# Second tap sums from superblock 10 on, and a tap sum tied to a later tile, in a dynamic convolution with a two-matmul block

## The chip, the cores and the metric

The kernel runs on one core of a Trainium2 chip. The metric is device time in microseconds (us) of one execution. The core has TensorE (PE, matmuls; PEld are its weight loads), VectorE (DVE), ScalarE (ACT), GpSimd (POOL) and SyncE (SP, which here only issues DMA transfers). GpSimd issues DMA transfers too. All transfers run on the same 16 DMA engines of the core.

## The reference

The first stage is a causal convolution with 7 taps whose weights differ by token and head (softmax over the taps); the second is two matmuls with `h - tanh(h)` between them.

```python
def _attn_ref(x, weight_gen):          # x: 8 x 4096 x 192; weight_gen: 8 x 4096 x 8 heads x 7 taps
    w = softmax of weight_gen over the 7 taps
    x_pad = np.concatenate([np.zeros((B, 6, D)), x], axis=1)
    x_unf = x_pad[:, idx, :]           # the 7 last tokens of each token, by head
    out = np.einsum('bshk,bskhg->bshg', w, x_unf)
...
def _moe_ref(x, w_in, w_out):          # x: 32768 x 192; w_in: 192 x 2048; w_out: 2048 x 192
    h = x @ w_in
    g = h - np.tanh(h)
    return g @ w_out
```

Inputs and output are float32.

## The kernel before, in words

The 32768 tokens are cut into 32 superblocks of 1024 tokens (8 tokens in each of 128 partitions). Stage n of the main loop (`for n in range(1, NTOT)`) is the time in which superblock n goes through the first matmul; it is cut into 16 f tiles of 128 columns, indexed 0 to 15. The program's order is written out by hand (`manual_schedule`): each engine runs its instructions in the order of the program, and waits only where data or a dependency added by `order` demands it.

**An f tile.** `gemm1(n, f)`: TensorE does 6 matmuls of 512 columns into `ph` (L478), ScalarE takes `tanh` of it (L491, `th`), VectorE subtracts (L492, `gt`). Between the f tiles TensorE does the second matmul of superblock n-1 in pieces (L546, `obank`), doled out by the plan's `pairs`; ScalarE copies its results out (L565), and SP stores them (`out_sb`, L569).

**The taps of a superblock.** `products(n + 2)` is called in stage n at f tile 1 and gives the seven tap products of superblock n+2. GpSimd multiplies taps 0 to 3 into a tile `pa` in two instructions (L263), later taps 4 to 6 into `pb` (L263). The tokens that VectorE takes off GpSimd (`help`, L291 and L263 on DVE: the last token of taps 0 and 1 at f tile 3 of stage n-2, and for superblocks 9 to 14 one more at f tile 12 of stage n-3) make the first of the two `pa` instructions shorter: 2688 elements with one token taken off, 2304 with two.

**Sums by DMA.** GpSimd then issues an adding DMA (`dma_sum`, L252) that adds `pb` to `pa[0:3]`; this is the three-tap sum, and four products are left. For the superblocks in `TWO_SUMS` (13 to 31) a second adding DMA adds `pa[2:4]` to `pa[0:2]`, and two products are left. It is issued by `second_sum(n - 1)` behind the `pa` products of the next superblock, and waits for the landing of the three-tap sum. The rest of the products (pb and the three-tap sum) is the function `rest`, called in stage n at the f tile of the last help (3). So GpSimd's queue for steady superblocks is: two `pa` products of m, second sum of m-1, `pb` product of m, three-tap sum of m, and the same for m+1.

**Transposes.** In stage n TensorE turns the products that are left of superblock n+1 by matmuls with a unit matrix that add them up in PSUM (`transposes`, `conv_sums`, L418, `pc`): 24 matmuls for each product. ScalarE copies the result to `convT` (L444), which stage n+1 needs from its first f tile on. The plan says where they stand: in `STEADY`, 32 of 48 (or 64 of 96) at f tile 13 and the rest at f tile 14 (`t2=(13, 0)`, `t1=(14, 8)`); in `DOUBLE`, used for stages 4 to 11, at f tiles 11 and 15.

**Loads.** `loads(n)` at f tile 1 issues from SP the x of superblock n+3 (`load_x`, L150; it waits for GpSimd's first `pa` product of superblock n+2 by `x_after`) and the tap weights of a later superblock (`load_wg`, L136). x lies in a ring of two places. SP's queue holds x loads, weight loads, out stores and, for each fourth superblock, a zero row for the halo (L160), each behind the one before.

Of the kernel before, what the change touches and what calls it, by code (L numbers as in the profile page):

```python
# [8 lines left out]
FP32 = mybir.dt.float32  # L9
# [7 lines left out]
def kernel(  # L17
# [8 lines left out]
    nc = tc.nc  # L26
# [5 lines left out]
    P = nc.NUM_PARTITIONS  # L32
    R = P // 2
# [5 lines left out]
    HT = TOK // 2  # L39
    NSB = S // TOK  # L40
    NTOT = B * NSB
    NFT = F // P
    NC = D // R
    KA, KH = 4, 2
    PART = (2, 3)
    TWO_SUMS = (13, 14, 15, 16, 17, 18, 19, 20, 21, 22, 23, 24, 25, 26, 27, 28, 29, 30, 31)
    THREE = ()
    AHEAD = 4
    STORE_FIRST = 8
    EXTRA = (5, 9, 11, 13)  # L50

    HELP = {n: ((n - 2, 3, 2),) for n in range(4, 32)} | {n: ((n - 2, 3, 2), (n - 3, 12, 2)) for n in range(9, 15)}
    CUTS0 = [0, 2, 4]
    LAST_TAP = (4, 5, 6, 7, 8)
    X_LATE = ()
# [24 lines left out]
    psum_h = ctx.enter_context(tc.tile_pool(name="psum_h", bufs=3, space=bass.MemoryType.PSUM))  # L80
    psum_o = ctx.enter_context(tc.tile_pool(name="psum_o", bufs=1, space=bass.MemoryType.PSUM))

    ident = const.tile([P, P], BF16, name="ident")
# [24 lines left out]
    last_sub = {}  # L108
# [5 lines left out]
    ramp_scale = {}  # L114
    tap_of = {}
    pace_of = {}

    def order(inst, other, reason):
        tc.add_manual_dep(
            inst.ins,  # L120
            other.ins.name,
            mybir.DependencyInfo(mybir.DependencyClass.Sync, mybir.DependencyReason.DATA),
            reason=reason,
        )
# [9 lines left out]
    def load_wg(n):  # L134
        wg_t = wgpool.tile([P, J, H, K], FP32, name="wg_t")
        nc.sync.dma_start(out=wg_t[:], in_=tokens(weight_gen.rearrange("b s h k -> (b s) h k"), n))  # L136
        wg_of[n] = wg_t

    def load_x(n, behind=None):

        wide = 2 * J if n < 2 else J
        at = {0: 0, 1: J}.get(n, 0 if n % 2 else HALO + J)
        if n == 2:
            x_t = npool.tile([P, 2 * J, D], FP32, name="x2", tag="spare")[:, 0 : HALO + J]
        else:
            x_t = x_ring[:, at : at + HALO + J]

        def rows(p0, p1, r0=0, r1=HALO + J):
            first = x[0, 0:1]
            return nc.sync.dma_start(  # L150
                out=x_t[p0:p1, r0:r1, :],
                in_=bass.AP(
                    tensor=first.tensor,
                    offset=first.offset + (n * TOK - (TOK - J if n == 1 else 0) + p0 * wide - HALO + r0) * D,
                    ap=[[wide * D, p1 - p0], [D, r1 - r0], [1, D]],
                ),
            )

        def no_halo():
            nc.sync.dma_start(  # L160
                out=x_t[0:1, 0:HALO, :],
                in_=zero[:].rearrange("o (h d) -> o h d", h=1).to_broadcast([1, HALO, D]),
            )

        if n == 0:
            rows(0, P, HALO, HALO + J)
            rows(16, P, 0, HALO)
            rows(1, 16, 0, HALO)
            no_halo()
        else:  # L170
            dma = rows(0, P, HALO if n == 1 else 0)
            if behind is not None:
                order(dma, behind, "order of the loads")
            if n % NSB == 0:
                halo_of[n] = no_halo
        x_of[n] = x_t
# [74 lines left out]
    def dma_sum(out, in_):  # L251
        return nc.gpsimd.dma_start(  # L252
            out=out.rearrange("p k j d -> p k (j d)"),
            in_=in_.rearrange("p k j d -> p k (j d)"),
            accum_op=mybir.AluOpType.add,
            max_dma_last_dim=2 * J * D,
        )
# [36 lines left out]
    def products(n, taps=None, sums=None, hooks={}):  # L294

        x_t = x_of.pop(n)
        wsm, wsm_v, e_t, zr = wsm_of.pop(n)
        if e_t is not None:
            scale(nc.gpsimd, wsm[:], e_t, zr[:])

        pa = held[n][2] if n in held else papool.tile([P, KA, J, D], BF16, name="pa")
        held[n] = (x_t, wsm, pa)
        if n == 1:

            last = [opool.tile([P, 2, J, D], BF16, name="pb1", tag="out_sb") for _ in range(2)]
            home = [(pa, 0, KA), (last[0], KA, KA + 2), (last[1], KA + 2, K)]
        else:
            pb = pbpool.tile([P, K - KA, J, D], BF16, name="pb")
            home = [(pa, 0, KA), (pb, KA, K)]

        def prod(k0, k1):
            for t, a, b in home:
                if a <= k0 and k1 <= b:
                    return t[:, k0 - a : k1 - a]

        def mul(eng, k0, k1, j0=0, j1=J):
            w = wsm_v if eng is nc.vector else wsm[:]
            return tap_product(eng, prod(k0, k1), x_t, w[:, j0:j1, :, k0:k1], (1, K), k0, k1, j0, j1)

        def parts(*ks):  # L320
            return [[prod(k, k + 1)[:, 0] for k in ks]] * NC

        if taps is not None:
            for eng, k0, k1, j0, j1 in taps:
                m = mul(eng, k0, k1, j0, j1)
                if eng is nc.vector:
                    tap_of.setdefault((n, k0), m)
                if j1 == 1:
                    first_halo[0] = m
                if k0 in hooks:  # L330
                    hooks[k0]()
            prods_of[n] = parts(*sums)
            return

        end = KA - 1 if n in LAST_TAP else KA
        left = [J - sum(kh > k for _, _, kh in HELP.get(n, ())) for k in range(KA)]
        for j, k in {(j, k) for j, k, _ in ACT_OPS.get(n, ())}:
            left[k] = min(left[k], j)

        def most(k0, k1):  # L340
            return mul(nc.gpsimd, k0, k1, 0, left[k0])

        cuts = [0, *(k for k in range(1, end) if left[k] != left[k - 1]), end]
        if cuts == [0, end]:
            cuts = sorted({*(c for c in CUTS0 if c <= end), end})
        first = None
        for k0, k1 in zip(cuts, cuts[1:]):
            m = most(k0, k1)
            first = first or m
        x_after[n + 1] = first  # L350
        second_sum(n - 1)
        def rest():
            if n in PART:
                dma_sum(pa[:, 0:2], pa[:, 2:4])
            if n - 1 in whole:
                mul(nc.gpsimd, KA, K - 1)
                third_sum(n - 1)
                mul(nc.gpsimd, K - 1, K)
            else:
                mul(nc.gpsimd, KA, K)  # L360
            if n in PART:
                prods_of[n] = parts(4, 5, 6, 0, 1)
            else:
                dma_sum(pa[:, 0:3], pb[:, 0:3])
                if n in LAST_TAP:
                    most(KA - 1, KA)
                if n in TWO_SUMS:
                    to_sum[n] = pa
                    prods_of[n] = parts(0, 1)
                else:  # L370
                    prods_of[n] = parts(3, 0, 1, 2)
                if n == NTOT - 1:
                    second_sum(n)
                    third_sum(n)

        return rest
# [277 lines left out]
    V, G_, A = nc.vector, nc.gpsimd, nc.scalar  # L654
    load_wg(0)
    load_x(0)
    load_wg(1)
    softmax_exp(0)
    for c0, c1 in W_CUTS:
# [89 lines left out]
    STEADY = dict(pairs=(5, 11, 0, 16, 4, 12, 6, 10, 0, 6, 10, 8, 8, 8, 8, 16), t1=(14, 8), t2=(13, 0), scale=14, sums=(1, 13))  # L749
    FIRST = dict(pairs=(4, 12, 0, 16, 1, 15, 0, 16, 0, 16, 0, 13, 3, 0, 16, 16), t1=(15, 2), t2=(11, 10), scale=15, sums=(1, 2, 3, 4, 8, 10))  # L750
    APART = dict(pairs=(4, 12, 0, 16, 0, 16, 4, 12, 0, 16, 4, 12, 0, 6, 10, 16), t1=(15, 5), t2=(10, 2), scale=15, sums=(7, 10))
    APART_IN = ()
    DOUBLE = dict(pairs=(5, 11, 0, 16, 0, 16, 6, 10, 0, 6, 10, 7, 9, 0, 16, 16), t1=(15, 6), t2=(11, 3), scale=15, sums=(1, 11))
    DOUBLE_IN = (4, 5, 6, 7, 8, 9, 10, 11)
    TURNED = dict(pairs=(5, 11, 0, 16, 3, 13, 6, 10, 0, 6, 10, 5, 11, 5, 11, 16), t1=(16, 0), t2=(16, 0), scale=14, sums=(1, 7))
    TURN_AT = 13

# [7 lines left out]
    def loads(n):  # L765
        if n + 3 < NTOT:
            load_x(n + 3, x_after.pop(n + 3, None))
        if n > 1:
            for m in range(wg_next[0], min(n + (5 if n >= AHEAD - 1 else 4) + 1, NTOT)):
                load_wg(m)  # L770
            wg_next[0] = min(n + (5 if n >= AHEAD - 1 else 4) + 1, NTOT)
# [4 lines left out]
    for n in range(1, NTOT):  # L776
        more = n < NTOT - 1
        finish = []
        turned = n + 1 in THREE
        plan = TURNED if turned else FIRST if n == 1 else DOUBLE if n in DOUBLE_IN else APART if n in APART_IN else STEADY  # L780

        soft = [m for m in (n + 3 if n <= AHEAD else n + 4,) if m < NTOT]
        for f in range(NFT):
            ph = gemm1(n, f)
# [29 lines left out]
            for m in (n + 2, n + 3):  # L814
                for j, k, h in [o for o, at in zip(ACT_OPS.get(m, ()), ACT_AT.get(m, ())) if at == (n, f)]:
                    act_product(m, j, k, h)
                for t, (a, b, kh) in enumerate(HELP.get(m, ())):
                    if (a, b) == (n, f):
                        help(m, ph, J - 1 - t, kh)
            if n + 2 < NTOT and f == (9 if n == 1 else max([b for a, b, _ in HELP.get(n + 2, ()) if a == n] + [3])):  # L820
                rest()
            if f == (9 if n == 1 else 1) and n > STORE_FIRST:
                loads(n)
# [21 lines left out]
            out_pairs(plan["pairs"][f] - done)  # L845
            if f == (9 if n == 1 else 1) and n <= STORE_FIRST:
                loads(n)

    gemm2_last(0, 0, J)
    out_pairs(NFT)  # L850
# [33 lines left out]
```

## Time and profile before

| | us |
|---|---|
| median of 3 runs | 746.12 (744.75 to 746.63) |
| the profiled execution | 745.19 |
| its span, first to last instruction | 743.3 |
| mean granted TensorE clock | 0.998 of full speed |

The profile is of one execution. A page gives busy time by engine, the chain of work that ended last, groups of instructions by source line, and the DMA queues; views of the trace give the same for a stretch of time, by tile, or as a timeline. In a timeline row the first number is the start in us from the span's start, the second the time that the merged instructions took; `[0.77 <-issue]` is idle time before it and what ended it, where "issue" stands for nothing that the profile shows. In a row of stretches, `a:b length` is followed by the busy time of each engine with its number of instructions, the granted clock, the busy share of the DMA engines and GB/s. In a row of DMA issues the last number is the median time from issue to landing. Line numbers are those of the kernel before.

### The profile page before, as it was taken

The page shows a single profiled execution, that of the slowest core. Times are in us where ns is not written, and L with a number is a line of the kernel's source. Part 1 is how long each engine was busy: PE and PEld are TensorE (multiplying, and loading weights), DVE is VectorE, ACT ScalarE, POOL GpSimd, SP SyncE. Part 2 cuts the span into 40 slices and gives each one's busy share as a digit, 9 for nine tenths or more (in the row PEclk, how much of TensorE's full clock was granted, in tenths as well). Part 3 has the DMA queues.
Part 4 walks back from the last instruction along what each step waited for, and adds up shares of the span by engine and source line. Part 5 has one row for each costly group of instructions (what it writes and reads, how often), then busy time and mean ns, then how long its engine had stood idle before and what let it go on. Part 6 is the DMA issues. An engine that isn't in the chain of part 4 may idle for free.

```text
span 743.3 us, 30036 instructions
## 1 busy us (share of the span) xinstructions
PE 720.6 (97%) x13616; PEld 553.4 (74%) x13616; DVE 687.2 (92%) x726; ACT 639.5 (86%) x871; POOL 653.5 (88%) x161
## 2 busy tenths in 40 slices
PE   3799999999999999999999999999999999999997
PEld 2477777777777777777777777777777777877777
DVE  7999999999999999999999999999999999988893
ACT  4888888988888888989888999898998989888882
POOL 7999999999999999999999999999999999991000
PEclk9999999999999999999999999999999999999999
DMA  7925366766567768977777987877887877776112
GB/s 204 245 46 161 140 192 161 194 180 155 123 181 184 184 183 221 230 188 200 168 195 207 236 187 203 184 191 205 218 215 192 199 175 192 191 149 110 45 45 86
DMA packets 34237, 129.47 MB, mean 174 GB/s; under 512 B 4559, under 2 KB 9407, under 8 KB 30270
## 3 DMA queue, kind: packets, MB, share of 16 engines
q0 software_dynamic: 19392, 51.12, 40.4%
q1 hardware_dynamic: 14718, 76.44, 27.5%
q8 instruction: 106, 1.74, 0.9%
q14 instruction: 21, 0.17, 0.1%
HBM read 53.93 MB, written 25.17 MB: 106 GB/s over the span
## 4 chain that ended last, share of the span: by engine, by line
PE 93%; DVE 4%; issue 1%; ACT 1%; DMA 0%; DVEq 0%
PE obank L546 44%; PE ph L478 44%; PE pc L418 4%; DVE gt L492 2%; PE po L589 1%; DVE pa L263 1%; ACT th L491 0%; DVE pb L263 0%; DMA wg_t<-in_weight_gen_dram 0%; DVE zsum L194 0%; DVE wsm L245 0%; DVE obank L222 0%; ACT convT L436 0%; ACT wg_t L180 0%; DVE obank L245 0%
## 5 line engine op out<-in xcount | busy, mean ns | idle before, releaser
L492 DVE TENSOR_TENSOR gt<-ph,th 128x1024 bf16<-128x1024 f32 x512 | 601.0, 1218 | 34.4 <-ACT th L491 24.0
L491 ACT ACTIVATE th<-ph 128x1024 f32<-128x1024 f32 x512 | 512.9, 1026 | 67.7 <-PE ph L478 57.5
L478 PE MATMUL ph<-convT,w_in 64*128 64x512 bf16 x3072 | 413.1, 378 | 5.0 <-DVE gt L492 3.7
L546 PEld LDWEIGHTS <-gt 64*128 64x128 bf16 x7936 | 354.4, 94 | 83.7 <-issue 9.2
L546 PE MATMUL obank<-w_out,gt 64*128 64x192 bf16 x7936 | 407.1, 243 | 2.5 <-issue 2.4
L263 POOL TENSOR_TENSOR pa<-x_ring,wsm 128x2688 bf16<-128x2688 f32 (+3 forms) x66 | 327.6, 5217 | 0.2
L263 POOL TENSOR_TENSOR pb<-x_ring,wsm 128x4608 bf16<-128x4608 f32 (+2 forms) x32 | 274.5, 8580 | 1.3 <-DVE wsm L245 1.2
L478 PEld LDWEIGHTS <-w_in 64*128 64x128 bf16 x3072 | 159.5, 94 | 85.7 <-issue 16.5
L565 ACT ACTIVATE out_sb<-obank 128x192 f32<-128x192 f32 x248 | 81.2, 328 | 11.0 <-PE obank L546 10.3
L444 ACT ACTIVATE convT<-pc 128x1024 bf16<-128x1024 f32 (+1 forms) x62 | 50.1, 810 | 5.3 <-PE pc L418 5.2
L252 POOL DMA_DIRECT2D pa<-pb x28 | 36.0, 1284 | 14.0 <-POOL pb L263 9.2
L418 PEld LDWEIGHTS <-pa 64*128 64x128 bf16 x2064 | 41.6, 100 | 6.8 <-POOL pa L263 1.4
L418 PE MATMUL pc<-ident,pa 64*128 64x64 bf16 x1968 | 41.3, 192 | 2.1 <-POOL pa L263 1.3
L252 POOL DMA_DIRECT2D pa<-pa x21 | 34.7, 1650 | 9.5 <-DMA pa<-pb 8.9
L194 DVE TENSOR_REDUCE zsum<-wg_t 128x32 f32<-128x224 f32 (+1 forms) x61 | 23.6, 387 | 2.9 <-ACT wg_t L180 2.9
L180 ACT ACTIVATE wg_t<-wg_t 128x448 f32<-128x448 f32 x32 | 18.2, 569 | 7.1 <-DMA wg_t<-in_weight_gen_dram 7.1
L263 DVE TENSOR_TENSOR pa<-x_ring,ph 128x384 bf16<-128x384 f32 x34 | 18.8, 554 | 2.0 <-DVE ph L291 0.3
L245 DVE TENSOR_TENSOR wsm<-wg_t,pc 128x448 f32<-128x448 f32 x27 | 16.8, 621 | 2.5
L209 DVE RECIPROCAL pc<-zsum 128x64 f32<-128x64 f32 x27 | 14.9, 550 | 0.0
L418 PE MATMUL pc<-ident,pb 64*128 64x64 bf16 x216 | 4.9, 206 | 9.2 <-POOL pb L263 9.2
L418 PEld LDWEIGHTS <-pb 64*128 64x128 bf16 x288 | 6.3, 107 | 9.7 <-POOL pb L263 9.2
L589 PE MATMUL po<-w_out,gt 64*128 64x192 bf16 x256 | 11.2, 243 | 0.0
(28 smaller groups left out, 75.3 us busy)
## 6 DMA issues: line engine op xcount, KB each, us to landing
x_ring<-in_x_dram SPq DMA_DIRECT2D x29, 1344.0 KB, 7.9
pa<-pb POOLq DMA_DIRECT2D x28, 1152.0 KB, 9.8
out_dram<-out_sb SPq DMA_DIRECT2D x31, 768.0 KB, 4.2
pa<-pa POOLq DMA_DIRECT2D x21, 768.0 KB, 7.4
wg_t<-in_weight_gen_dram SPq DMA_DIRECT2D x32, 224.0 KB, 7.1
x_ring<-in_x_dram SPq DMA_DIRECT2D x2, 768.0 KB
x<-in_x_dram SPq DMA_DIRECT2D x1, 1344.0 KB
w_out<-in_moe_w_out_dram POOLq DMA_DIRECT2D x1, 768.0 KB, 9.4
```

The lines of the kernel that those rows point to most:

```text
L180: last_exp[0] = nc.scalar.activation(out=wg_t[:].rearrange("p j h k -> p (j h k)"), in_=wg_t[:].rearrange("p j h k -> p (j h k)"), func=AC ...
L194: nc.vector.reduce_sum(out=zsum_of[n][:, j0 * H : j1 * H], in_=e_of[n][:, j0:j1].rearrange("p j h k -> p (j h) k"), axis=AX.X,)
L252: return nc.gpsimd.dma_start(out=out.rearrange("p k j d -> p k (j d)"), in_=in_.rearrange("p k j d -> p k (j d)"), accum_op=mybir.AluOpTyp ...
L263: return eng.tensor_mul(bass.AP(tensor=out.tensor, offset=out.offset + j0 * D, ap=[out.ap[0], [J * D, nk], [G, run], [1, G]]), bass.AP(ten ...
L418: nc.tensor.matmul(pc[r][:, col : col + R] if home else pc[:, r, col : col + R], lhsT=prods[c][gi][r * R : (r + 1) * R, 2 * j : 2 * j + 2] ...
L444: last_conv[0] = nc.scalar.activation(out=out, in_=pc[:, :, 0:cols].rearrange("p r (cj t) -> p r cj t", t=R), func=ACT.Copy,)
L478: nc.tensor.matmul(ph[:, r, :], lhsT=w_in[r * R : (r + 1) * R, c, ff], rhs=convT[r * R : (r + 1) * R, c, :], start=(c == 0), stop=(c == NC ...
L491: last_act[0] = nc.scalar.activation(out=th[:], in_=ph_f, func=ACT.Tanh)
L492: last_sub[0] = nc.vector.tensor_sub(gt[:], ph_f, th[:])
L546: mm = nc.tensor.matmul(po[:, 0:D], lhsT=g_of[n][f][r * R : (r + 1) * R, col : col + P], rhs=w_out[r * R : (r + 1) * R, f, :], start=(r == ...
L565: last_act[0] = nc.scalar.activation(out=out_sb[:, j, :], in_=po[:, 0:D], func=ACT.Copy)
L589: nc.tensor.matmul(po[:, r, 0:D], lhsT=g_of[n][f][r * R : (r + 1) * R, col : col + P], rhs=w_out[r * R : (r + 1) * R, f, :], start=(f == 0 ...
```

## The change

`TWO_SUMS` begins at superblock 10 instead of 13. VectorE's second token is left to superblocks 9 and 10 alone. The plan `DOUBLE` ends with stage 8; stages 9 to 11 use `STEADY`. For superblocks 14 to 31 `rest` is called at f tile 10 and its three-tap sum gets a dependency on the last subtract issued by then. Weight loads are issued at f tile 9, apart from the x loads. `WARM`, `SUM_LATE`, `SUM_BEHIND` and `LATE_FROM` are set so that their branches do nothing.

```diff
-    TWO_SUMS = (13, 14, 15, 16, 17, 18, 19, 20, 21, 22, 23, 24, 25, 26, 27, 28, 29, 30, 31)
+    TWO_SUMS = tuple(range(10, 32))
...
-    HELP = {n: ((n - 2, 3, 2),) for n in range(4, 32)} | {n: ((n - 2, 3, 2), (n - 3, 12, 2)) for n in range(9, 15)}
+    WG_AT = 9
+    LOCK, LOCKED = 10, tuple(range(14, 32))
+    WARM = 0
+    SUM_LATE, SUM_BEHIND = (), ()
+    HELP = {n: ((n - 2, 3, 2),) for n in range(4, 32)} | {n: ((n - 2, 3, 2), (n - 3, 12, 2)) for n in (9, 10)}
...
-                dma_sum(pa[:, 0:3], pb[:, 0:3])
-                if n in LAST_TAP:
+                def first_sum():
+                    dma = dma_sum(pa[:, 0:3], pb[:, 0:3])
+                    if n in LOCKED:
+                        order(dma, last_sub[0], "place of the transfer")
...
-    DOUBLE_IN = (4, 5, 6, 7, 8, 9, 10, 11)
+    DOUBLE_IN = tuple(range(4, 9))
...
+        if WG_AT is None:
+            weights(n)
+
+    def weights(n):
         if n > 1:
             for m in range(wg_next[0], min(n + (5 if n >= AHEAD - 1 else 4) + 1, NTOT)):
                 load_wg(m)
...
-            if n + 2 < NTOT and f == (9 if n == 1 else max([b for a, b, _ in HELP.get(n + 2, ()) if a == n] + [3])):
+            if n + 2 < NTOT and f == (9 if n == 1 else LOCK if n + 2 in LOCKED else max([b for a, b, _ in HELP.get(n + 2, ()) if a == n] + [3])):
                 rest()
...
             if f == (9 if n == 1 else 1) and n <= STORE_FIRST:
                 loads(n)
+            if f == WG_AT:
+                weights(n)
```

More of the change, by code (lines that the diff above doesn't have):

```diff
@@ L116 @@
     pace_of = {}
+    sum_of = {}
     def order(inst, other, reason):
@@ L348, in products @@
             m = most(k0, k1)
+            if first is None and n - 1 in sum_of:
+                sum_of.pop(n - 1)()
             first = first or m
@@ L363, in rest @@
             else:
-                dma_sum(pa[:, 0:3], pb[:, 0:3])
-                if n in LAST_TAP:
-                    most(KA - 1, KA)
+                def first_sum():
+                    dma = dma_sum(pa[:, 0:3], pb[:, 0:3])
+                    if n in LOCKED:
+                        order(dma, last_sub[0], "place of the transfer")
+                if n in LAST_TAP and n in SUM_BEHIND:
+                    most(KA - 1, KA)
+                    first_sum()
+                elif n in SUM_LATE:
+                    sum_of[n] = first_sum
+                else:
+                    first_sum()
+                    if n in LAST_TAP:
+                        most(KA - 1, KA)
                 if n in TWO_SUMS:
@@ L656 @@
     load_x(0)
+    if WARM:
+        warm = psum_h.tile([P, 2, HT], FP32, name="warm", tag="ph")
+        for i in range(WARM):
+            nc.tensor.matmul(warm[:, 0, 0:R], lhsT=ident[0:R], rhs=ident[0:R, 0:R], start=True, stop=True)
     load_wg(1)
@@ L753 @@
     DOUBLE = dict(pairs=(5, 11, 0, 16, 0, 16, 6, 10, 0, 6, 10, 7, 9, 0, 16, 16), t1=(15, 6), t2=(11, 3), scale=15, sums=(1, 11))
-    DOUBLE_IN = (4, 5, 6, 7, 8, 9, 10, 11)
+    LATE, LATE_FROM = STEADY, 99
+    DOUBLE_IN = tuple(range(4, 9))
     TURNED = dict(pairs=(5, 11, 0, 16, 3, 13, 6, 10, 0, 6, 10, 5, 11, 5, 11, 16), t1=(16, 0), t2=(16, 0), scale=14, sums=(1, 7))
@@ L779 @@
         turned = n + 1 in THREE
-        plan = TURNED if turned else FIRST if n == 1 else DOUBLE if n in DOUBLE_IN else APART if n in APART_IN else STEADY
+        plan = TURNED if turned else FIRST if n == 1 else DOUBLE if n in DOUBLE_IN else APART if n in APART_IN else LATE if n >= LATE_FROM else STEADY
         soft = [m for m in (n + 3 if n <= AHEAD else n + 4,) if m < NTOT]
```

## The prediction

> **What bounds the kernel now.** I read the page first: engine times, the chain of work that ended last, the DMA queues.
>
> ```profile
> span 743.3 us, 30036 instructions
> PE 720.6 (97%) x13616; PEld 553.4 (74%) x13616; DVE 687.2 (92%) x726; ACT 639.5 (86%) x871; POOL 653.5 (88%) x161
> PE 93%; DVE 4%; issue 1%; ACT 1%; DMA 0%; DVEq 0%
> q8 instruction: 106, 1.74, 0.9%
> ```
>
> TensorE is 97% busy and carries 93% of the chain, so time is won by giving it less to do or by closing its gaps. Then I cut the span into stages, each from VectorE's first subtract of superblock n (f tile 0) to that of n+1. The first row below is stage 8, the next eight are stages 9 to 16, then 17 to 23, 24 to 27, 28 to 30.
>
> ```profile
> core 0: us, PE busy (x) PEld busy (x) DVE busy (x) ACT busy (x) POOL busy (x), PEclk, DMA share, GB/s
> 197.90:220.46 22.56, 22.56 (x454) 17.22 (x450) 21.54 (x25) 19.94 (x28) 22.26 (x5) 1.00 0.74 182
> 220.46:243.27 22.81, 22.80 (x456) 17.16 (x452) 21.54 (x25) 20.01 (x28) 22.51 (x6) 1.00 0.79 184
> 243.27:266.84 23.57, 22.80 (x454) 18.27 (x450) 21.67 (x25) 19.92 (x28) 23.27 (x6) 1.00 0.79 204
> 266.84:289.88 23.04, 22.66 (x452) 17.38 (x448) 21.55 (x25) 19.91 (x27) 22.74 (x6) 1.00 0.73 197
> 289.88:311.75 21.87, 21.87 (x406) 16.63 (x402) 21.05 (x23) 19.72 (x28) 21.57 (x6) 1.00 0.82 205
> 311.75:334.32 22.57, 21.91 (x406) 16.87 (x402) 21.04 (x23) 19.76 (x27) 22.18 (x6) 1.00 0.82 202
> 334.32:356.18 21.86, 21.86 (x406) 16.86 (x402) 21.04 (x23) 19.71 (x27) 20.67 (x6) 1.00 0.78 196
> 356.18:378.04 21.86, 21.08 (x392) 16.18 (x387) 21.04 (x24) 19.71 (x27) 21.16 (x6) 1.00 0.81 200
> 378.04:400.90 22.86, 22.86 (x415) 18.22 (x416) 21.14 (x24) 19.71 (x28) 21.65 (x6) 1.00 0.79 196
> 400.90:554.01 153.11, 153.11 (x2806) 117.74 (x2802) 147.34 (x156) 137.96 (x190) 149.70 (x36) 1.00 0.81 202
> 554.01:642.45 88.44, 88.04 (x1607) 67.27 (x1603) 84.22 (x90) 79.26 (x108) 85.94 (x21) 1.00 0.80 196
> 642.45:708.00 65.55, 65.55 (x1206) 51.26 (x1203) 58.00 (x53) 58.08 (x79) 29.41 (x8) 1.00 0.47 104
> ```
>
> The reader sees two bare lengths, at full clock: 22.56 where four products are transposed (stage 8, no gap), 21.86 where two are (stage 14, no gap). Everything above is excess: stages 9 to 11 hold 0.25 + 1.01 + 0.48 = 1.74 over 22.56; stage 13 0.71, stage 16 1.00, stages 17 to 23 153.11 - 7 x 21.86 = 0.09, stages 24 to 27 1.00 over 21.86, together 2.80. Sum 4.54 us. The timeline of TensorE shows what part of it is:
>
> ```profile
> 247.10 0.57 PE L546 MATMUL obank<-w_out,gt 64*128 64x192 bf16 x9 [0.77 <-issue]
> 286.72 0.60 PE L418 MATMUL pc<-ident,pa 64*128 64x64 bf16 x29 [0.38 <-issue]
> 328.65 0.42 PE L546 MATMUL obank<-w_out,gt 64*128 64x192 bf16 x6 [0.66 <-issue]
> 378.04 0.32 PE L546 MATMUL obank<-w_out,gt 64*128 64x192 bf16 x3 [0.78 <-issue]
> 638.18 0.32 PE L546 MATMUL obank<-w_out,gt 64*128 64x192 bf16 x3 [0.18 <-issue]
> ```
>
> No semaphore ends these gaps. Counting TensorE's instructions in order of start, the five stand at places 9153, 10689, 12225, 14017 and 23489: each 193 past a multiple of 256. The queue row fits: 1.74 MB over 27232 instructions is 64 bytes each, over 106 packets 256 instructions each. So I read them as late blocks of instructions, which share the DMA engines with x, sums and stores. [...]
>
> **The change part by part.** Base: the profiled execution's own 745.19 us.
>
> (1) Superblocks 10 to 12 get a second sum, so stages 9 to 11 transpose two products instead of four.
>
> ```profile
> L418 PE MATMUL pc<-ident,pa x96: 187/191/208, 210.7 to 217.7; 64*128 64x64 bf16 x96
> L418 PE MATMUL pc<-ident,pa x48: 189/190/191, 349.5 to 352.3; 64*128 64x64 bf16 x48
> ```
>
> That is 48 transposes less per stage, worth 22.56 - 21.86 = 0.70: -2.1 us, nothing hides it. The steady plan that comes with it starts the transposes 349.5 - 334.32 = 15.2 into the stage, later than the double plan's 210.7 - 197.90 = 12.8.
>
> (2) VectorE's second token goes for superblocks 11 to 14. VectorE has 22.56 - 21.54 = 1.0 to spare in such a stage, so its saving is worth nothing. GpSimd takes the token over, and issues three more sums:
>
> ```profile
> 196.32 1.29 POOL L252 DMA_DIRECT2D pa<-pb  x1 [0.30 <-POOL pb L263]
> 216.08 1.28 POOL L252 DMA_DIRECT2D pa<-pb  x1 [0.30 <-POOL pb L263]
> 296.34 1.28 POOL L252 DMA_DIRECT2D pa<-pb  x1 [0.30 <-POOL pb L263]
> 297.15 11.01 POOL L263 TENSOR_TENSOR pa<-x_ring,wsm 128x2688 bf16<-128x2688 f32 x2
> 307.63 1.72 POOL L252 DMA_DIRECT2D pa<-pa  x1
> 318.11 1.28 POOL L252 DMA_DIRECT2D pa<-pb  x1 [0.39 <-POOL pb L263]
> 340.69 1.28 POOL L252 DMA_DIRECT2D pa<-pb  x1 [1.19 <-DVE pa L263]
> ```
>
> GpSimd's round was 216.08 - 196.32 = 19.76 with one sum and two tokens taken off it; with two sums and one token it is 318.11 - 296.34 less 0.09 of extra wait = 21.68. Against stages of 21.86 it now gains 0.18 a stage, where it gained 2.8. This is the cover, and it is thin.
>
> (3) What is late next: superblock 10's first sum is issued at 216.08 as before. Its second follows after 307.63 - 296.34 = 11.29, at 227.4. Transposes want it at 220.46 + 15.2 = 235.7.
>
> ```profile
> pa<-pa POOLq DMA_DIRECT2D x21, 768.0 KB, 7.4
> 221.69 0.33 SPq L150 DMA_DIRECT2D x_ring<-in_x_dram  x1
> 223.47 0.71 SPq L569 DMA_DIRECT2D out_dram<-out_sb  x1
> 224.50:232.00 7.50, 7.50 (x127) 5.43 (x124) 7.33 (x8) 6.70 (x9) 7.50 (x2) 1.00 0.97 317
> 508.40:512.70 4.30, 4.30 (x71) 3.15 (x67) 4.20 (x6) 3.77 (x6) 4.30 (x1) 1.00 1.01 179
> ```
>
> With a median landing it is there at 234.8: no wait. But x and the store, issued before, fill the engines until 232.0 (share 0.97). If it moves only after them, its own 4.3 us (share 1.01; the landing follows about 1 later) end at 237.3: 1.6 late. Bounds 0 and 1.6 for stage 9; I take 1.3, since the earlier transfers are already queued. A wait of TensorE lets GpSimd catch up by as much, so stages 10 and 11 pay about nothing. +1.3 us.
>
> (4) The lock. In the built order the three-tap sum of superblock m (14 to 31) waits for the subtract of the tile with index 10 of stage m-2, the eleventh; before, for VectorE's help at index 3 (the 1.19 above).
>
> ```profile
> 340.06 10.64 DVE L492 TENSOR_TENSOR gt<-ph,th 128x1024 bf16<-128x1024 f32 x9
> ```
>
> The nine are tiles 4 to 12; the seventh ends at 340.06 + 7 x 1.18 = 348.3, 14.0 into the stage, and with 0.5 from event to issue (as at 340.69) the sum goes at 14.5. GpSimd comes later anyway: superblock 11's sum at 216.08 + 21.68 = 237.8 is 17.3 into stage 9, and 0.18 a stage plus what TensorE waits in (3) brings it to 14.5 near stage 16. From there the lock holds it, 0.18 a stage, with the next superblock's products, its second sum and the next pb product queued behind. Who waits for those are the transposes: second sum at 14.5 + 11.3 - 21.86 = 3.9, landed at 11.3 with the median 7.4, wanted at 15.2. Cover 3.9; cost nothing.
>
> (5) What the lock gives. A block of 256 instructions lasts 7.7 us in plain work (704 instructions in 21.19) and 5.5 with all 48 transposes in it (160 such instructions, plus 0.67): the next block, asked for around 10 to 13, has the least time. Before, the first sum's packets ran then (issued 6.4 in, landing 9.8 later) and x behind them. After, the sum starts at 14.5 to 17.3, x about 6 behind it, so that 11.3 to 14.5 is empty once locked. I expect most of the 4.54 to go. Bounds of what stays: 0 and 4.54; I take 1.0, for stages 9 to 15 where the second sum still ends near 15. Net -3.5.
>
> (6) Weight loads now stand behind the out store in SP's queue (no wait for f tile 9 is built in; where a halo row is zeroed, behind that too). 224 KB, issued some 2 us into a stage and used by ScalarE in the next one: covered by over 10 us, 0. It takes them out of the stretch behind x.
>
> Sum: 745.19 - 2.1 + 1.3 - 3.5 = 740.9. The three runs' median lies 0.93 above the profiled execution; gaps that come and go are one source of such spread, and I add half of it: 741.3.
>
> **The rivals.**
> (A) The gaps stay: the blocks are late for another reason, or meet the moved transfers elsewhere. For it: DMA shares stay near 0.8 of every stage, and the store, x and second sum bunch up to 11 in. Against: the gaps come only in blocks with little time. 745.19 - 2.1 + 1.3 = 744.4, within noise. [...]
> (B) Slower: GpSimd becomes the bound. Its second sum waits for the first one's landing, then all behind it slips.
>
> ```profile
> pa<-pb POOLq DMA_DIRECT2D x28, 1152.0 KB, 9.8
> pa<-pb POOLq DMA_DIRECT2D x1, 1152.0 KB, 12.0
> ```
>
> The median 9.8 fits in 11.29; the 12.0 (issued at 131.4, a store beside it) does not. At 12.0 the round is 21.68 + 0.71 = 22.39, 0.53 a stage over 21.86 for the 21 stages from 9 on: +11.1, with the gaps hidden beneath it: 745.19 - 2.1 - 4.54 + 1.3 + 11.1 = 751.0. It binds from a landing of 11.5 on (0.18 spent) and makes the kernel slower than before by over 0.3% from 11.9 on. Against: the moved sum starts when the store is long out.
> (C) The change doesn't do what it says: GpSimd never reaches the lock (any round above 21.8) and second sums land near 15 to the end, with some gaps and waits left. 741.3 + 1.5 = 742.8.
>
> **How the numbers follow.** Forecast 0.52 (739 to 742.5), C 0.14, A 0.21, B 0.13. Less than 0.3% (2.2 us around 746.12, 743.9 to 748.4) is what the measurement can't tell from no change. Forecast, C and a quarter of A are faster: 0.71. The rest of A and a little of B are the same: 0.17. Slower 0.12. The range 738.6 (all gaps gone, no wait in stage 9: 745.19 - 2.1 - 4.54) to 745.6 leaves out B and tails of some 0.06.
>
> **What would show it.** Right: 48 transposes and about 21.9 in stages 9 to 11, a wait on the second sum at the transposes of stage 9 alone, first sums creeping from 17 to 14.5 and then released by VectorE's gt, fewer issue gaps from stage 12. Wrong: stages all a few tenths over 21.86 with waits on the sums' landing (B), or as many issue gaps as before (A).

## The result, and the profile after

The kernel after takes 741.54 us (median, 741.23 to 741.66), the kernel before 746.30 us (744.75 to 746.63) beside it; the ratio is 0.9947 [0.9933, 0.9960]. The profiled execution of the kernel after took 741.6 us with a span of 739.5; by the trace the span went from 743.34 to 739.46, 3.9 us less. Line numbers below are those of the kernel after: L257 is the adding DMA, L268 the products, L436 the transposes, L510 `gt`, L564 the second matmul. In `after_store_help`, which has some lines more, L512 is `gt`, L270 the products, and L438 the transposes.

First the page of the kernel after: span, engines, chain, the queue of instruction blocks, and the medians from issue to landing.

```profile
span 739.5 us, 29740 instructions
PE 717.7 (97%) x13472; PEld 551.4 (75%) x13472; DVE 684.7 (93%) x718; ACT 638.5 (86%) x871; POOL 660.1 (89%) x164
PE 64%; POOL 24%; DVE 4%; issue 4%; DMA 2%; ACT 0%; SPq 0%; POOLq 0%; DVEq 0%
q8 instruction: 105, 1.72, 1.0%
pa<-pb POOLq DMA_DIRECT2D x28, 1152.0 KB, 9.9
pa<-pa POOLq DMA_DIRECT2D x24, 768.0 KB, 9.7
```

TensorE has 144 matmuls less (13616 to 13472), the 48 transposes of three stages. GpSimd now holds 24% of the chain, because the chain runs back from a wait of TensorE into GpSimd's queue. The packets of the instruction queue are one fewer (105); what changed is when they come. The first sums still land after 9.9 us; the second sums take 9.7 instead of 7.4. Next the stretches: stages 8, 9, 10, 11, then 12 to 27 in one row, then 28 to 30.

```profile
core 0: us, PE busy (x) PEld busy (x) DVE busy (x) ACT busy (x) POOL busy (x), PEclk, DMA share, GB/s
198.63:221.11 22.48, 22.48 (x454) 17.33 (x450) 21.06 (x24) 19.93 (x27) 22.18 (x5) 1.00 0.74 183
221.11:244.47 23.36, 21.94 (x406) 17.00 (x402) 21.03 (x22) 19.83 (x27) 23.06 (x7) 1.00 0.88 202
244.47:267.22 22.75, 21.93 (x406) 16.85 (x402) 21.04 (x23) 19.87 (x27) 22.45 (x6) 1.00 0.88 203
267.22:289.08 21.86, 21.86 (x406) 16.93 (x402) 21.05 (x23) 19.71 (x27) 21.56 (x6) 1.00 0.85 203
289.08:638.76 349.68, 349.68 (x6406) 269.58 (x6402) 336.57 (x354) 315.28 (x433) 341.85 (x81) 1.00 0.84 201
638.76:704.25 65.49, 65.49 (x1206) 50.50 (x1202) 57.92 (x53) 58.04 (x78) 37.98 (x10) 1.00 0.60 134
```

In the row of stages 12 to 27 TensorE's busy time equals the length: 349.68 us, and 16 x 21.86 is 349.76. Not one of the gaps of before is left there. Only stages 9 and 10 are longer than their work, and TensorE's timeline says for what it waits:

```profile
237.91 0.65 PE L436 MATMUL pc<-ident,pa 64*128 64x64 bf16 x32 [1.42 <-DMA pa<-pa]
260.66 0.65 PE L436 MATMUL pc<-ident,pa 64*128 64x64 bf16 x32 [0.82 <-DMA pa<-pa]
```

Both are first transposes of a stage that wait for the second sum. The 3.9 us of the span divide so, from the stage bounds of both kernels: 0.65 more up to stage 9; 67.97 instead of 69.42 in stages 9 to 11, 1.45 less; 349.68 instead of 352.57 in stages 12 to 27, 2.89 less; 0.2 less behind. The 0.65 is not of the change: in the run `before_lock10` below, which differs from before only from stage 12 on, stage 9 also begins at 221.28 (before: 220.46).

Why stage 10 waits too is seen in GpSimd's timeline,

```profile
227.95 1.43 POOL L257 DMA_DIRECT2D pa<-pa  x1
238.06 1.28 POOL L257 DMA_DIRECT2D pa<-pb  x1 [0.30 <-POOL pb L268]
249.35 1.72 POOL L257 DMA_DIRECT2D pa<-pa  x1
259.74 1.28 POOL L257 DMA_DIRECT2D pa<-pb  x1 [0.30 <-DVE gt L510]
281.42 1.28 POOL L257 DMA_DIRECT2D pa<-pb  x1 [0.30 <-DVE gt L510]
303.57 1.28 POOL L257 DMA_DIRECT2D pa<-pb  x1 [0.77 <-DVE gt L510]
```

and in SP's queue (x, the store, the weights):

```profile
244.34 0.33 SPq L155 DMA_DIRECT2D x_ring<-in_x_dram  x1
246.21 0.34 SPq L587 DMA_DIRECT2D out_dram<-out_sb  x1
246.59 1.71 SPq L141 DMA_DIRECT2D wg_t<-in_weight_gen_dram  x1
```

The second sum of stage 9 is issued at 227.95, 6.84 into the stage; that of stage 10 at 249.35, only 4.88 into it, so GpSimd did catch up by 2.0. But x, store and weights went out ahead of it, and the transposes got it 11.3 later, at 260.66. The first sums (`pa<-pb`) stand 16.95, 15.27, 14.20 and 14.49 into stages 9 to 12: the lock, released by VectorE's `gt`, is reached in stage 12, where GpSimd stands idle 0.77 before the sum. The 0.30 in the rows before is its usual pause behind the `pb` product; those superblocks (12 and 13) have no lock, whatever releaser the row names.

### The profile page after: what moved, and what is told of

Read it like the earlier page. It is cut to its first block, busy times and chain, and to the rows that moved or that the text cites. A ratio compares the mean times of both kernels' runs of the same rounds, so it can differ in the third digit from the quotient of the medians.

```text
span 739.5 us, 29740 instructions
## 1 busy us (share of the span) xinstructions
PE 717.7 (97%) x13472; PEld 551.4 (75%) x13472; DVE 684.7 (93%) x718; ACT 638.5 (86%) x871; POOL 660.1 (89%) x164
## 4 chain that ended last, share of the span: by engine, by line
PE 64%; POOL 24%; DVE 4%; issue 4%; DMA 2%; ACT 0%; SPq 0%; POOLq 0%; DVEq 0%
PE obank L564 31%; PE ph L496 30%; POOL pa L268 13%; POOL pb L268 10%; DVE gt L510 3%; PE pc L436 2%; DMA pa<-pa 2%; PE po L607 1%; DMA x_ring<-zero 1%; POOL pa L257 1%; DVE pa L268 1%; POOL wsm L250 0%; ACT th L509 0%; DVE zsum L199 0%; SPq L155 0%
## 5 line engine op out<-in xcount | busy, mean ns | idle before, releaser
L510 DVE TENSOR_TENSOR gt<-ph,th 128x1024 bf16<-128x1024 f32 x512 | 601.0, 1218 | 33.1 <-ACT th L509 23.4
L564 PEld LDWEIGHTS <-gt 64*128 64x128 bf16 x7936 | 354.5, 94 | 81.4 <-issue 6.0
L564 PE MATMUL obank<-w_out,gt 64*128 64x192 bf16 x7936 | 406.5, 243 | 0.1
L268 POOL TENSOR_TENSOR pa<-x_ring,wsm 128x2688 bf16<-128x2688 f32 (+3 forms) x66 | 330.3, 5258 | 0.3
L268 POOL TENSOR_TENSOR pb<-x_ring,wsm 128x4608 bf16<-128x4608 f32 (+2 forms) x32 | 276.1, 8630 | 1.3 <-DMA x_ring<-in_x_dram 1.2
L496 PEld LDWEIGHTS <-w_in 64*128 64x128 bf16 x3072 | 159.6, 94 | 84.1 <-issue 16.5
L257 POOL DMA_DIRECT2D pa<-pa x24 | 39.4, 1642 | 9.3 <-DMA pa<-pb 8.6
L257 POOL DMA_DIRECT2D pa<-pb x28 | 36.0, 1284 | 11.6 <-POOL pb L268 10.3
L436 PEld LDWEIGHTS <-pa 64*128 64x128 bf16 x1920 | 39.6, 101 | 9.1 <-POOL pb L268 1.9
L436 PE MATMUL pc<-ident,pa 64*128 64x64 bf16 x1824 | 39.1, 193 | 3.8 <-DMA pa<-pa 2.2
L268 DVE TENSOR_TENSOR pa<-x_ring,ph 128x384 bf16<-128x384 f32 x30 | 16.6, 554 | 1.8 <-DMA x_ring<-in_x_dram 0.5
L214 DVE RECIPROCAL pc<-zsum 128x64 f32<-128x64 f32 x27 | 14.9, 550 | 0.0
L436 PE MATMUL pc<-ident,pb 64*128 64x64 bf16 x216 | 4.9, 206 | 9.2 <-POOL pb L268 9.2
L436 PEld LDWEIGHTS <-pb 64*128 64x128 bf16 x288 | 6.3, 107 | 9.7 <-POOL pb L268 9.2
L607 PE MATMUL po<-w_out,gt 64*128 64x192 bf16 x256 | 11.2, 243 | 0.0
```

Source lines behind the costliest of these rows:

```text
L257: return nc.gpsimd.dma_start(out=out.rearrange("p k j d -> p k (j d)"), in_=in_.rearrange("p k j d -> p k (j d)"), accum_op=mybir.AluOpTyp ...
L268: return eng.tensor_mul(bass.AP(tensor=out.tensor, offset=out.offset + j0 * D, ap=[out.ap[0], [J * D, nk], [G, run], [1, G]]), bass.AP(ten ...
L436: nc.tensor.matmul(pc[r][:, col : col + R] if home else pc[:, r, col : col + R], lhsT=prods[c][gi][r * R : (r + 1) * R, 2 * j : 2 * j + 2] ...
L496: nc.tensor.matmul(ph[:, r, :], lhsT=w_in[r * R : (r + 1) * R, c, ff], rhs=convT[r * R : (r + 1) * R, c, :], start=(c == 0), stop=(c == NC ...
L510: last_sub[0] = nc.vector.tensor_sub(gt[:], ph_f, th[:])
L564: mm = nc.tensor.matmul(po[:, 0:D], lhsT=g_of[n][f][r * R : (r + 1) * R, col : col + P], rhs=w_out[r * R : (r + 1) * R, f, :], start=(r == ...
```

## The experiments

Each time stands beside that of the kernel before on the same chip.

**The lock alone, at three places.** The code of the change with every setting of before, and the three-tap sums of superblocks 14 to 31 tied to the f tile with index 10, 6 or 12.

```diff
+    LOCK, LOCKED = 10, tuple(range(14, 32))     # before_lock10
+    LOCK, LOCKED = 6, tuple(range(14, 32))      # before_lock6
+    LOCK, LOCKED = 12, tuple(range(14, 32))     # before_lock12
```

> The kernel before with the lock alone (three-tap sums of superblocks 14 to 31 wait for f tile 10). Place theory: gaps of late instruction blocks from stage 13 on (2.8 us of the 4.5) go, stages 9 to 11 stay as before: 743.3. Rival, only the transposes taken out count: 746.

> The kernel before with the lock at f tile 6. First sums then go at about 9.8 us into a stage, packets from 11.5 to 18.5, x behind them: across the blocks asked for at 10 to 15. Place theory: gaps as before or more from stage 13 on, 746 to 749. Rival, any lock helps by evenness alone: 743.3 as with f tile 10.

> The kernel before with the lock at f tile 12. First sums go at 16.8, second ones at 6.2 into the next stage, landing 9.9 later at 16.1 where the transposes want them at 15.2. Few gaps, but a wait of about 0.45 us in each of 17 stages, since the lock keeps GpSimd from catching up: 751. Rival, GpSimd's slack absorbs it: 743.3.

| lock | first sums issued at, into the stage | us | before | ratio |
|---|---|---|---|---|
| 10 | 14.5 | 743.36 | 745.01 | 0.9978 [0.9968, 0.9987] |
| 6 | 9.8 | 748.61 | 745.97 | 1.0037 [1.0022, 1.0051] |
| 12 | 16.9 | 758.12 | 745.97 | 1.0160 [1.0136, 1.0183] |

The work is the same in all three; only the place of the first sum is set differently, and the times lie 14.8 us apart. The second sum and x stand behind it in GpSimd's order and move with it: x goes out about 12.7 into the stage in the kernel before, 16.1 with the lock at 6, 20.8 with 10. With the lock at 10, TensorE keeps the first two gaps of before, in stages 10 and 11, where no superblock is locked yet, and stages 12 to 29 become nearly bare. Its timeline, and its stretch of stages 12 to 27:

```profile
247.78 0.57 PE L564 MATMUL obank<-w_out,gt 64*128 64x192 bf16 x9 [0.77 <-issue]
287.39 0.59 PE L436 MATMUL pc<-ident,pa 64*128 64x64 bf16 x29 [0.37 <-issue]
```

```profile
290.55:640.60 350.05, 349.96 (x6406) 269.02 (x6402) 336.66 (x352) 315.48 (x432) 334.31 (x79) 1.00 0.83 195
```

That is 0.29 above 349.76, where before had 2.80. The 0.29 is no late block: stage 24 is 0.31 over the bare length, and its only idle time, 0.09, is that of a matmul 6.2 us into it which waits for VectorE's `pa` product. At 6 the gaps are worse than before: stages 12 to 27 take 355.21 us (290.63 to 645.84), 5.45 of excess. At 12 the gaps are gone from stage 12 on, but second sums are issued up to 2.4 later than with 10, and TensorE waits at the transposes, 0.2 to 2.0 us in 12 of 17 stages. Stage 13:

```profile
329.89 0.81 PE L436 MATMUL pc<-ident,pa 64*128 64x64 bf16 x32 [2.02 <-DMA pa<-pa]
```

Stages 12 to 27 take 364.43 us there, 14.67 of excess. The direction was foreseen; the size was not. The landing takes as long as with the lock at 10 (10.9 and 10.5 us in stage 13), so the delay goes to the transposes almost whole.

**The second sums without the lock, from either side.** `before_early` is before with the change's `TWO_SUMS`, help list and plan; `after_no_lock` is the kernel after without the lock (the first has the weights with x).

```diff
     # before_early
+    TWO_SUMS = tuple(range(10, 32))
+    HELP = {n: ((n - 2, 3, 2),) for n in range(4, 32)} | {n: ((n - 2, 3, 2), (n - 3, 12, 2)) for n in (9, 10)}
+    DOUBLE_IN = tuple(range(4, 9))
     # after_no_lock
-    LOCK, LOCKED = 10, tuple(range(14, 32))
+    LOCK, LOCKED = 10, ()
```

> The kernel before with the early second sums, the shorter help list and the steady plan in stages 9 to 11, without lock and with the weight loads beside x. Place theory: 2.1 us less of transposes, 2.2 us of waits for second sums in stages 9 and 10, and since GpSimd's first sums now come at 14 to 17 by themselves and drift back by only 0.2 a stage, most gaps go without any lock: 742 to 743. Rival, the lock is what removes the gaps: 2.8 us of them stay, 745 to 746.

> The changed kernel without the lock. Place theory: first sums creep from 14.2 us into stage 11 to about 11 in stage 28, their packets start 1.7 later, so few gaps come back, late in the kernel: 741.5 to 743. Rival, the lock carries the gain: 744 or more.

`before_early`: 746.36 beside 745.01, 1.0011 [0.9991, 1.0032]. `after_no_lock`: 746.74 (742.33 to 748.60) beside 745.01, 1.0006 [0.9981, 1.0030]. By their medians neither gains, so in the median it is the lock that carries the gain, not the early second sums by themselves. In the profiled execution of `after_no_lock` stages 9 to 15 are bare, then gaps come back in 16 and 23 to 26; stages 23, 24 and 25, with the largest gap and the first sums there:

```profile
530.54:553.16 22.62, 21.99 (x402) 16.54 (x396) 21.04 (x24) 19.91 (x27) 22.06 (x6) 1.00 0.84 208
553.16:576.34 23.18, 21.31 (x395) 16.07 (x395) 21.09 (x24) 19.91 (x27) 22.41 (x7) 1.00 0.83 208
576.34:600.06 23.72, 23.00 (x418) 18.33 (x415) 21.17 (x22) 19.72 (x27) 23.42 (x8) 1.00 0.79 192
```

```profile
575.99 0.57 PE L564 MATMUL obank<-w_out,gt 64*128 64x192 bf16 x9 [1.15 <-issue]
```

```profile
542.38 1.28 POOL L257 DMA_DIRECT2D pa<-pb  x1 [0.56 <-POOL pb L268]
564.54 1.28 POOL L257 DMA_DIRECT2D pa<-pb  x1 [0.77 <-DVE gt L510]
586.23 1.28 POOL L257 DMA_DIRECT2D pa<-pb  x1 [0.30 <-POOL pb L268]
```

The first sums stand 11.84, 11.38 and 9.89 into these stages. GpSimd gains about 0.17 a stage, as predicted (14.29 in stage 9, 13.61 in stage 13), and each gap of TensorE lets it gain more. Both profiled executions had lost time earlier, which put GpSimd ahead from the start: some 3 us in stage 3 here (of that below), and 4.3 us in stage 9 of `before_early`, whose first sums then stand at 12.7 in stage 10.

The medians hide a spread. Four of the ten times of `after_no_lock` are 742.3 to 742.9, which is 2.1 to 2.7 below the kernel before and about what was expected of a kernel that needs no lock; the other six are 745.9 to 748.6, and the profiled one is of these. So without the lock the gain is sometimes half there. What the traces show of the lock is that it keeps an early loss from growing: `after_store_9_10` (below) has the lock and lost as much in stage 3, and its stages 12 to 27 take 349.66 us, against 354.76 in `after_no_lock`. What the four shorter executions looked like is not shown.

**Are the gaps late instruction blocks?** 64 small matmuls whose result nobody uses stand at the start of before: 128 instructions, half a block.

```diff
+    for i in range(64):
+        nc.tensor.matmul(warm[:, 0, 0:R], lhsT=ident[0:R], rhs=ident[0:R, 0:R], start=True, stop=True)
```

> The kernel before with 64 small matmuls (128 TensorE instructions) ahead of the first transposes, their result unused. Block theory: the gaps still stand 193 past a multiple of 256 in TensorE's count, so in other stages and at other matmuls than before; total of gaps 2 to 7 us. Rival, the gaps belong to places of the kernel: stages 10, 11, 13, 15 again, within 0.1 us of their places.

The time is the same, 745.99 beside 745.97, 0.9992 [0.9976, 1.0007]. The gaps move. Three of its six in TensorE's timeline:

```profile
108.26 0.24 PE L564 MATMUL obank<-w_out,gt 64*128 64x192 bf16 x1 [0.57 <-issue]
266.71 0.59 PE L436 MATMUL pc<-ident,pa 64*128 64x64 bf16 x29 [1.17 <-issue]
286.43 0.82 PE L496 MATMUL ph<-convT,w_in 64*128 64x512 bf16 x6 [0.66 <-issue]
```

By count they stand at places 3777, 9921 and 10689, again each 193 past a multiple of 256 though every instruction has moved by 128: other instructions, other points of the stage (22.4, 20.7 and 16.6 in), the same boundary. So the gap belongs to the boundary of a block, not to an instruction.

With this the waits of the blocks can be read from the packets of the instruction queue, each of 16384 bytes, which is 256 instructions of 64: the time from TensorE's first instruction of one block to the start of the packet that brings the next. In the kernel before it goes from -1.0 to 4.9 us, and each packet ended 1.26 us or more ahead of its block's first instruction, so a block came while the one ahead of it ran, or up to 1.0 us sooner. The five gaps of the prediction ended 1.35 to 1.56 us behind the end of a packet. "Asked for" names the start of the block ahead, here and in the prediction; what sends a packet off is not shown. The table has the blocks of stages 12 to 27 that were asked for 10 to 16.5 us into a stage; the transposes make these the shortest, 5.3 us at the least.

```
kernel          first sums at   blocks   median wait   longest wait
before          6.4 to 7.4        16        3.25          4.43
before_lock6    9.8 to 10.8       17        3.09          4.42
after_no_lock   7.2 to 13.8       16        3.21          4.97
before_early    7.0 to 12.3       16        3.79          4.65
before_lock10   14.5 to 15        17        0.50          3.05
after           14.5 to 15.1      16        0.28          1.36
```

A packet takes about 0.95 us and TensorE ran its first instruction no sooner than 1.24 us behind it, so a block of 5.3 us is late from a wait of about 3.1 on. In the kernel after the long waits (up to 5.1) fall on blocks of 6.85 to 8.2 us.

What the packets wait behind is seen in the share of the DMA engines. The stretch from 13 to 16 us into stage 14, before and after (the share is the last number but one):

```profile
347.32:350.32 3.00, 3.00 (x79) 2.43 (x76) 2.92 (x3) 2.62 (x4) 3.00 (x1) 1.00 1.01 245
345.80:348.80 3.00, 3.00 (x80) 2.44 (x77) 2.92 (x3) 2.61 (x4) 2.28 (x3) 1.00 0.03 5
```

With the lock at 6 the same stretch has 1.06, with 10 it has 0.02. In the kernel before, six of the eleven waits over 3 us in these blocks pass while the first sum moves, the other five while x moves; with the lock at 6 it is nearly all the first sum. So no single transfer is at fault: the lock at 10 puts all of them outside this stretch.

**The weights.** The kernel after, with the weights issued with x as before.

```diff
-    WG_AT = 9
+    WG_AT = None
```

> The changed kernel with the weight loads issued with x again. They are 224 KB and used a stage later: 741.5 to 742. Rival, moving them is what cleared the gaps: 743 or more.

742.37 beside 745.97, 0.9952 [0.9936, 0.9969]. There is no gap behind stage 9, so the place of the weights is not what cleared them. The times fall into two groups, 741.3 to 741.8 and 743.0 to 743.9; the profiled execution belongs to the second, and the last section shows what it met.

**Stage 10's wait.** In `after_store_late` the out stores of superblocks 8 and 9 are taken from their places. The kernel leaves these two stores out, one in stage 10 and one in stage 11.

```diff
+    STORE_LATE, STORE_AT = (8, 9), 6
...
+            if n in STORE_LATE:
+                late_store[n] = store
+            else:
+                store()
```

> The changed kernel, with the out stores of superblocks 8 and 9 issued behind f tile 6 of stages 9 and 10 instead of near 2 us. If the second sums of superblocks 10 and 11 are late because the store and x stand before them in the DMA engines, the two waits of the transposes (1.42 and 0.82 us) shrink to 0.3 or less: 739.5. If they are late because GpSimd issues them late, nothing moves: 741.5.

741.31 beside 745.01, 0.9955 [0.9945, 0.9966]; with two stores missing the time itself says little. Stage 10 is what it was for:

```profile
244.23:266.08 21.85, 21.85 (x406) 16.93 (x402) 21.03 (x23) 19.71 (x27) 21.55 (x7) 1.00 0.73 168
```

The second sum was issued no earlier (5.1 into the stage, against 4.9), and nothing waits for it: it landed 7.0 us after its issue, where it took 11.2. So the store ahead of it is needed for stage 10's wait. Stage 9, where the store remained, still waited 1.54.

**Mending stages 9 and 10.** `after_store_9_10` holds the stores of superblocks 7 and 8 back to f tile 9 of stages 9 and 10 (all stores are made); `after_help_12` leaves VectorE's second token to superblocks 9 to 12; `after_store_help` does both.

```diff
+    STORE_LATE, STORE_AT = (7, 8), 9
-    ... for n in (9, 10)}
+    ... for n in range(9, 13)}
```

> The changed kernel, with the out stores that go near 2 us into stages 9 and 10 (superblocks 7 and 8) held behind f tile 9 there. If the second sums of superblocks 10 and 11 land late because the store stands before them in the DMA engines: no wait in stage 10, under 0.3 us in stage 9 (the second sum lands near 14.5 instead of 16.7), 739.5. If x alone, or GpSimd's late issue, is the cause: stage 9 still waits over 1 us and the time is 741 or more.

> The changed kernel with VectorE's second token kept for superblocks 11 and 12 too. GpSimd's second sum of superblock 10 goes 0.6 us earlier, that of 11 1.2. If the issue by GpSimd sets the landing: stage 9 waits 0.8 instead of 1.4, stage 10 none, 740.2. If the queue of x and the store ahead sets it: stage 9 as before the edit (1.4 to 1.5), 741 to 741.5.

> Both edits together: no wait of the transposes in stages 9 and 10, no issue gap after stage 8: 739 to 739.5, the bare length of all stages. If the held stores bring new gaps to the instruction blocks of stages 9 and 10: 740 or more.

| | us | before | ratio |
|---|---|---|---|
| after_store_9_10 | 741.73 | 744.45 | 0.9966 [0.9954, 0.9979] |
| after_help_12 | 740.45 | 744.45 | 0.9949 [0.9936, 0.9963] |
| after_store_help | 740.36 | 744.45 | 0.9950 [0.9937, 0.9964] |

`after_store_9_10` decides nothing about the store: its stages 9 and 10 are bare (21.86, 21.85), but its profiled execution lost 3.1 us in stage 3, which put GpSimd ahead by as much. `after_help_12` shortens both waits (stretches of stages 9 and 10):

```profile
221.19:244.01 22.82, 21.92 (x406) 17.00 (x402) 21.68 (x25) 19.86 (x27) 22.42 (x7) 1.00 0.89 207
244.01:266.11 22.10, 21.93 (x406) 16.86 (x402) 21.04 (x23) 19.76 (x27) 21.80 (x6) 1.00 0.90 210
```

In `after_store_help` no transpose waits for a sum any more, and stage 9 is hardly shorter (22.73). The second sum of stage 9, issued 6.5 into the stage against 6.8, landed 6.6 us after its issue where `after_help_12` has 9.4, and the two kernels differ only in the held stores; so the store delays the sum in stage 9 too. TensorE now waits just behind these transposes for VectorE:

```profile
236.43 0.65 PE L438 MATMUL pc<-ident,pa 64*128 64x64 bf16 x32
238.55 0.82 PE L498 MATMUL ph<-convT,w_in 64*128 64x512 bf16 x6 [0.81 <-DVE pa L270]
```

```profile
226.99 10.63 DVE L512 TENSOR_TENSOR gt<-ph,th 128x1024 bf16<-128x1024 f32 x9
237.66 0.19 DVE L298 COPY ph<-wsm 128x16 f32<-128x16 f32 x1
237.94 0.55 DVE L270 TENSOR_TENSOR pa<-x_ring,ph 128x384 bf16<-128x384 f32 x1
```

VectorE worked without a break here, and its second token (0.75) stands between two subtracts, so the next `ph` comes free late. In `after_help_12` the wait for the sum, 0.90, lay over this one. That is why the two edits together are worth no more than one: a second limit stands right behind the first. The last two versions beat before; their ratios don't tell them from the change itself.

## Why the prediction was right, and where its steps were not

741.54 lies 0.2 from the 741.3 predicted, but two of the terms were off, (3) by 1.1 and (5) by 1.0, and cancelled. The other two differences, the 0.65 of stages that the change doesn't reach and the 0.4 that the prediction added for spread, also nearly agree by chance. So the nearness of the sum is in good part luck. Against the 745.19 of the profiled execution:

| step | predicted | measured |
|---|---|---|
| (1) 48 transposes less in stages 9 to 11 | -2.1 | -2.1 |
| (3) second sums late | +1.3 | +2.4 |
| (5) late blocks | -3.5 | -4.5 |
| (6) weights | 0 | 0 (stage 3 open) |
| stages before the change reaches them | | +0.65 |

(1) Right. TensorE's own work in the three stages is 21.94, 21.93 and 21.86; the -2.1 is three times the 0.70 between the bare lengths.

(2) Right in the main: without the lock, first sums creep forward by 0.17 a stage. But "its saving is worth nothing" holds only while something else is late in the same stage: the token that `after_store_help` keeps in stage 9 costs TensorE 0.81.

(3) The mechanism was right and its size was not. Stage 9 is 1.50 above 21.86 (1.3 taken, 1.6 the bound), and stage 10 is 0.89 above where the text had "about nothing". What failed is the step from GpSimd's catching up to "stages 10 and 11 pay about nothing". GpSimd did catch up, by 2.0, but in stage 10 the second sum did not land in time for it, because the store, x and weights were queued ahead; without the store the wait is gone. VectorE's second token also counts here: `after_help_12` issued its second sums at the same points of the stages, but x went out 0.4 earlier, behind a shorter first product, and the waits fell from 1.42 and 0.82 to 0.90 and 0.17. That x is the cause is an inference; the two were not changed apart.

(4) The lock is reached in stage 12, not "near stage 16", since TensorE's 2.4 us put GpSimd ahead. It cost nothing, but the cover is not 3.9: the second sum went out 3.6 to 4.5 into the stage and was there at 13.1 to 14.9 for transposes at 15.2. The cover is 0.3 to 2.1. The landing of 7.4 was taken from a kernel in which that sum ran elsewhere. `before_lock12` shows how near the edge is: two f tiles more, and 12 us are lost.

(5) Right, and larger: nothing is left of the 4.54, where 1.0 was to stay. But not all of it is the lock's, as the prediction had it: 1.74 lay in stages 9 to 11, before the lock is reached, and went with the early second sums and the steady plan (`before_lock10` keeps the gaps there, `after_no_lock` has none). And not all of it was late blocks: stage 9 (0.25) shows no gap, and stage 24 (0.30) only a wait for VectorE. The reading as late blocks is shown by the half block of added matmuls. That the place of the first sum, and of what follows it, decides is shown by the locks at 6 and 10. The prediction had the wrong window, though: not blocks asked for at 10 to 13 with the stretch 11.3 to 14.5 empty, but those asked for at 10 to 16.5. In the kernel after the DMA engines stand nearly idle from about 12.5 to 16.4 into a stage (share 0.06 in stage 14), since the packets of a sum issued at 14.5 begin 1.85 us later. In these runs a block's single packet waited up to 4.97 us among the blocks of the table, and TensorE up to 1.51 us for one (in stage 3 of `after_store_9_10`).

(6) No cost in the stages that the prediction looked at. In stage 3 the weights are wanted soon after they go out, in both kernels (issued at 79.3 and used at 85.75 before, 79.5 and 86.12 after), not 10 us later. ScalarE waited there for their landing in `after_no_lock` (1.58) and `after_store_9_10` (1.35), TensorE behind it, and a late block followed: 3 us. In `after_help_12` ScalarE waited there for 0.53, and in `after_weights_x`, where the weights go with x, for 0.45; none of the profiled versions built on before shows such a wait. Whether the change makes this loss likelier stays open.

Rival A fell: the gaps went. B fell: in stages 9 to 29 first sums landed after 9.1 to 11.1, under the 11.3 that the second ones allow, and no second sum waited for one there. Its mechanism exists: in `after_store_9_10` one first sum landed after 12.2, and the second sum waited 0.64 for it. C fell: the lock is reached and holds.

## What to carry to other kernels

Gaps of an engine that no semaphore ends, and that always stand at the same place modulo 256 instructions, were late blocks of instructions here; count places before looking for a dependency. They were closed by moving large transfers to where the shortest block is not being fetched. A lock on a compute tile did that for every stage from 12 to 27 (first sums 14.5 to 15.1 into it), while GpSimd's queue left to itself drifted through good and bad places (13.8 to 7.2 in `after_no_lock`), from wherever an earlier loss had put it. Work out the room on both sides before placing it: 9.8 us into the stage lost 2.6 us here, 14.5 gained 1.7, and 16.9 lost 12.

## What the runs showed of the hardware that was not expected

In three runs a wait of 2.0 to 2.6 us at the transposes cost more than itself. In `after_weights_x` stage 9 waited 2.12 us for the second sum, and the stage took 25.72, 3.86 above the bare 21.86. The stretches around it, with the granted clock third from the end:

```profile
238.70:239.70 1.00, 1.00 (x43) 1.00 (x44) 0.39 (x2) 0.41 (x1) 1.00 (x2) 0.78 0.00 0
239.70:240.70 1.00, 1.00 (x14) 0.77 (x11) 0.00 (x0) 0.61 (x1) 1.00 (x2) 0.50 0.50 96
241.70:242.70 1.00, 1.00 (x17) 1.00 (x15) 0.00 (x0) 0.97 (x1) 1.00 (x1) 0.52 1.07 184
242.70:243.70 1.00, 1.00 (x30) 0.72 (x28) 0.92 (x1) 0.83 (x3) 1.00 (x1) 1.00 1.13 200
```

The clock is halved for 3.41 us, which costs 1.74 us (TensorE is busy for 23.60 us in that stage, in a bare one for 21.86): 2.12 + 1.74 is the 3.86. The two groups of times of that kernel lie 1.9 apart, near to this; that this wait is what parts them is likely, but no execution of the shorter group was profiled. `before_early` (2.57) and `before_lock12` (2.02, stage 25.61) show the same; a wait of 1.74 in `before_lock12` (stage 23.66) and the 1.42 of the kernel after do not. Changes of the clock lie whole multiples of 3.41 us apart in a run (from 20.80 to 239.26 in `after_weights_x`, 64 times; from 13.03 to 743.48 in the kernel before, 214 times), and each of these five waits lay inside one step of 3.41 us, counted from them; what a wait across two steps costs, no run shows. Of the five, the longest with the clock at 1.00 is 1.74 us and the shortest with a halved one 2.02, which cost 3.75. So the 1.42 us in stage 9 of the kernel after is 0.3 us short of the one and 0.6 of the other, where a wait cost nearly twice its length.
